# One step of Q computed from one tile on GpSimd, another instruction order, and another order of the first loads

## Chip, cores and metric

The kernel runs on one NeuronCore of a Trainium2 chip. The metric is the device time of one execution in microseconds; lower is better. The engines are TensorE (PE, matrix products, with its weight loads shown as PEld), VectorE (DVE), ScalarE (ACT), GpSimd (POOL) and SyncE (SP, which issues transfers).

## What is computed

An attention over pooled keys, then two MLPs, all in float32. There are 12288 tokens and 128 channels; 768 keys; the MLPs have 2048 hidden units.

```python
kv_pool = kv.reshape(B, H // r, r, W // r, r, C).mean(axis=(2, 4))
k = v = kv_pool.reshape(B, -1, C) @ w_sr          # 768 keys
s = scale * (q @ k.transpose(0, 2, 1))
a = np.exp(s - s.max(-1, keepdims=True)); a /= a.sum(-1, keepdims=True) + 1e-09
x = a @ v
...
r = np.maximum(x @ w1_in, 0.0)                    # first MLP
y = (r * r) @ w1_out
...
h = y @ w2_in; h2 = h * h; h3 = h2 * h            # second MLP
P = a[0] + a[1] * h + a[2] * h2 + a[3] * h3
Q = 1.0 + np.abs(b[0]) * np.abs(h) + np.abs(b[1]) * h2
out = (P / (Q + 1e-06)) @ w2_out
```

## The kernel before

**Tiles.** Channels lie on the 128 partitions and tokens along the row. The tokens are cut into 25 blocks: one of 384, 22 of 512, one of 384 and one of 256. Hidden units are taken 128 at a time (16 rows of hidden units in a block), and the second MLP takes two of them together as a *pair*: 8 pairs in a block, 200 in all, each of 1024 columns in a full block.

**Three-part products.** Where a product needs float32 accuracy, an operand is split into a rounded high part and the low rest (names ending in h or H, and l or L), and three matmuls are added: high by high, high by low, low by high (L805 to L807 for the hidden products of both MLPs, L823 to L825 for some of the output products, L749 to L751 for attention). The other output products are plain float32 (L819), of which the trace has two records for each matmul. L679 are the scores, L720 the transposes of the softmax rows.

**Start.** Sixteen loads bring the keys' samples into one large buffer, `room`; DVE (L482) and POOL (L486) sum 16 samples a key. Small loads bring a and b. DVE decides from them by a flag whether a branch with completed squares (`SQUARES`, `fast=True`) can be taken; it is the one that runs. All engines read the flag and branch. DVE also works out the coefficients (columns of `cf`, 13 small steps), and the weights, which come as float64, are decoded on DVE (L574 to L592).

**Second MLP, a pair.** ACT takes |h| into U (L944) and a square of h into Z (L958). Q, divided by |b1|, goes into K. For the pairs in `qpool` POOL makes it in two steps, `kk` (L947) K = sU + t, and `qp` (L949) K = K · U; for the other pairs ACT squares (L952, `sq2`). ACT then takes ln (L969) and exp (L970) for an approximate 1/Q, and DVE does the cubic (L960), and three steps that refine and multiply (L982, L984, L987). Pairs 0 and 3 are split into mH (ACT or DVE, L997 or L998) and mL (POOL, L1000) for three-part output products.

**First MLP, a row.** Relu on ACT or DVE (L847, L850), the square on ACT or POOL (L853, L856), and for 10 of 16 rows a split, gH on ACT (L865) and gL on POOL (L871). `split` (L782, L779, L785) makes the high and low part of each block's x and y.

**What sets the order.** A planner, `Plan`, is run when the program is built. It has every operation with a priority (16 slots a block, offsets `off` by kind of operation, `lead1` and `leada` for how far the first MLP and attention run ahead), engine alternatives with a penalty in slots (`sq_act`, `sq_pool` and so on), a cost function for each, and the number of buffers and PSUM banks; it plays the work through by these costs and writes the instructions in the order of its starts. Each engine then runs its own instructions in that order.

## Time and profile before

| | |
|---|---|
| median of 3 runs | 1487.1 us (1486.95 to 1488.85) |
| the profiled execution | 1486.91 us, its span 1484.7 us |
| mean granted clock of TensorE | 0.989 |
| instructions in the trace | 18746 |
| TensorE busy | 1439.5 us |
| VectorE, ScalarE, GpSimd busy | 1386.9, 1393.4, 1334.1 us |

The time of an execution is the span of its instructions and about 2 us around it. An engine's busy time is the union of its instructions. A wait counts for the end only where the engine that waits sets the pace at that time; the chain that ended last, which the page follows back from the last instruction, lies on PE for 67% of the span.

### The profile page before, as it was taken

The page shows a single profiled execution, that of the slowest core. Times are in us where ns is not written, and L with a number is a line of the kernel's source. Part 1 is how long each engine was busy: PE and PEld are TensorE (multiplying, and loading weights), DVE is VectorE, ACT ScalarE, POOL GpSimd, SP SyncE. Part 2 cuts the span into 40 slices and gives each one's busy share as a digit, 9 for nine tenths or more (in the row PEclk, how much of TensorE's full clock was granted, in tenths as well). Part 3 has the DMA queues.
Part 4 walks back from the last instruction along what each step waited for, and adds up shares of the span by engine and source line. Part 5 has one row for each costly group of instructions (what it writes and reads, how often), then busy time and mean ns, then how long its engine had stood idle before and what let it go on. Part 6 is the DMA issues. An engine that isn't in the chain of part 4 may idle for free.

```text
span 1484.7 us, 18746 instructions
## 1 busy us (share of the span) xinstructions
PE 1439.5 (97%) x5991; PEld 1053.8 (71%) x5991; DVE 1386.9 (93%) x1857; ACT 1393.4 (94%) x2318; POOL 1334.1 (90%) x1021
## 2 busy tenths in 40 slices
PE   5999999999999999999999999999999999999986
PEld 4887767766767777776777777777777777767764
DVE  7999999999999999999999999999989899989998
ACT  3789989999999999999999999999999999999996
POOL 4789999998999899999998997989999999889984
PEclk8999999999999999999999999999999999999998
DMA  7310000000000000000000000000000000000000
GB/s 283 114 36 8 13 0 15 14 2 8 15 8 15 8 3 13 15 8 8 8 15 8 1 15 15 8 8 15 8 8 8 8 13 1 11 5 3 8 8 12
DMA packets 15549, 28.62 MB, mean 19 GB/s; under 512 B 1745, under 2 KB 6737, under 8 KB 15441
## 3 DMA queue, kind: packets, MB, share of 16 engines
q1 hardware_dynamic: 15440, 27.34, 5.5%
...
## 4 chain that ended last, share of the span: by engine, by line
PE 67%; POOL 13%; ACT 8%; DVE 7%; issue 3%; DMA 1%; SPq 0%; POOLq 0%; ACTq 0%; DVEq 0%
PE psum L819 17%; PE psum L805 9%; PE psum L806 8%; PE psum L807 8%; PE psum L679 4%; PE psum L824 4%; POOL room L949 4%; PE psum L825 4%; PE psum L823 4%; PE psum L720 4%; POOL gL L871 3%; POOL room L947 2%; POOL room L856 2%; PE psum L750 1%; PE psum L749 1%
## 5 line engine op out<-in xcount | busy, mean ns | idle before, releaser
L949 POOL TENSOR_TENSOR room<-room 128x1024 f32<-128x1024 f32 (+2 forms) x150 | 348.3, 2322 | 3.6
L871 POOL TENSOR_TENSOR gL<-room,gH 128x512 fp32r<-128x512 f32 (+2 forms) x250 | 313.0, 1262 | 20.8 <-PE psum L824 15.8
L960 DVE SCALAR_TENSOR_TENSOR room<-room,cf,psum 128x512 f32<-128x512 f32 (+2 forms) x400 | 279.5, 720 | 17.4 <-ACT room L958 15.8
L819 PE MATMUL psum<-room,w1o 128*128 128x512 f32 (+2 forms) x600 | 285.2, 583 | 4.0 <-DVE room L987 4.0
L856 POOL TENSOR_TENSOR room<-room 128x512 f32<-128x512 f32 (+2 forms) x261 | 262.3, 1022 | 12.5 <-ACT room L847 6.6
L982 DVE SCALAR_TENSOR_TENSOR room<-room,v,psum 128x1024 f32<-128x1024 f32 (+2 forms) x200 | 246.1, 1232 | 21.2 <-ACT psum L970 19.4
L958 ACT ACTIVATE room<-psum,cf 128x512 f32<-128x512 f32 (+2 forms) x400 | 262.8, 688 | 0.0
L969 ACT ACTIVATE room<-room,cf 128x1024 f32<-128x1024 f32 (+2 forms) x200 | 226.3, 1132 | 25.4 <-POOL room L949 24.8
L984 DVE SCALAR_TENSOR_TENSOR psum<-room,cf,psum 128x1024 f32<-128x1024 f32 (+2 forms) x200 | 247.5, 1238 | 0.0
L987 DVE SCALAR_TENSOR_TENSOR room<-psum,room 128x1024 f32<-128x1024 f32 (+2 forms) x200 | 235.2, 1177 | 3.1
L944 ACT ACTIVATE room<-psum 128x512 f32<-128x512 f32 (+2 forms) x400 | 223.4, 593 | 12.5 <-PE psum L807 6.5
L947 POOL TENSOR_SCALAR room<-room,cf 128x1024 f32<-128x1024 f32 (+2 forms) x150 | 164.7, 1098 | 48.3 <-ACT room L944 36.0
L970 ACT ACTIVATE psum<-room 128x1024 f32<-128x1024 f32 (+2 forms) x200 | 202.7, 1015 | 0.7 <-DVE room L960 0.3
L805 PE MATMUL psum<-yh,w1h 128*128 128x512 f32 (+2 forms) x400 | 191.2, 478 | 4.8 <-DVE room L987 3.5
L805 PE MATMUL psum<-xh,w0h 128*128 128x512 f32 (+2 forms) x400 | 182.8, 457 | 1.6 <-DVE xh L782 1.2
L819 PEld LDWEIGHTS psum<-room,w1o 128*128 128x128 f32 x600 | 111.1, 192 | 63.1 <-issue 42.9
L806 PE MATMUL psum<-xl,w0h 128*128 128x512 f32 (+2 forms) x400 | 153.4, 383 | 1.5 <-DVE xl L785 1.2
L807 PE MATMUL psum<-yh,w1l 128*128 128x512 f32 (+2 forms) x400 | 154.2, 386 | 0.0
L806 PE MATMUL psum<-yl,w1h 128*128 128x512 f32 (+2 forms) x400 | 153.9, 385 | 0.0
L807 PE MATMUL psum<-xh,w0l 128*128 128x512 f32 (+2 forms) x400 | 153.6, 384 | 0.0
L847 ACT ACTIVATE room<-psum 128x512 f32<-128x512 f32 (+2 forms) x255 | 148.3, 601 | 5.1 <-PE psum L807 3.2
L865 ACT ACTIVATE gH<-room 128x512 fp32r<-128x512 f32 (+2 forms) x250 | 149.8, 632 | 2.9 <-POOL room L856 2.6
...
## 6 DMA issues: line engine op xcount, KB each, us to landing
...
```

Of the source, the lines that this page charges most:

```text
L805: nc.tensor.matmul(out=out, lhsT=w_hi[m][:, sl], rhs=hi, start=True, stop=False)
L806: nc.tensor.matmul(out=out, lhsT=w_hi[m][:, sl], rhs=lo, start=False, stop=False)
L807: nc.tensor.matmul(out=out, lhsT=w_lo[m][:, sl], rhs=hi, start=False, stop=True)
L819: nc.tensor.matmul(out=o, lhsT=w_o[m][:, place[m][fi], :], rhs=rhs(), start=first, stop=last)
L856: nc.gpsimd.tensor_tensor(out=G(), in0=G(), in1=G(), op=ALU.mult)
L871: nc.gpsimd.tensor_tensor(out=mk("gL", gl)[:, :T], in0=G(), in1=f(tiles[gh][:, :T]), op=ALU.subtract)
L949: one("qp", POOL, c_pool, lambda v: nc.gpsimd.tensor_tensor(out=v(ku), in0=v(ku), in1=v(uu), op=ALU.mult), None, [uu], [ku])
L958: one("sP", ACT, ptr(c_actp), lambda v: act(out=v(zz), in_=v(hh), func=AF.Square, bias=co["c"]), "Z", [hh])
L960: one("z3", DVE, ptr(c_dve), lambda v: stt(out=v(zz), in0=v(zz), scalar=co["nd"], in1=v(hh), op0=ALU.subtract, op1=ALU.mult), None, [hh], ...
L982: one("g0", DVE, ptr(c_dve), lambda v: stt(out=v(zz), in0=v(zz), scalar=e0, in1=v(yy), op0=ALU.add, op1=ALU.mult), None, [yy], [zz])
L984: one("tt", DVE, c_dl, lambda v: stt(out=v(yy), in0=v(ku), scalar=dl, in1=v(yy), op0=ALU.add, op1=ALU.mult), None, [ku], [yy])
L987: one("g2", DVE, c_dve, lambda v: stt(out=v(g_), in0=v(yy), scalar=2.0, in1=v(zz), op0=ALU.subtract, op1=ALU.mult, reverse0=True), None, [ ...
```

## The change

It has four parts. First, in the branch that runs, POOL's two steps on Q become K = √QS · U + k1 and K = K · K, a linear step times itself; what is missing from Q is one constant, `da`, which ACT's ln and DVE's refinement add as they added another constant, `dp`, before. ACT's version of Q already had this form, so `da` now serves all pairs, and two coefficients are not needed any more. Second, the last two blocks have a set of pairs of their own that POOL takes (`qtail`): 0, 3, 4, 5, 6, 7, where the other blocks have 0, 1, 3, 4, 5, 7. Third, the planner has a cost of its own for the new step and a floor for three-part products, and nearly all of its numbers (buffers, banks, leads, penalties, offsets) are others. Fourth, ScalarE's queue issues b, a and `wsr`, so that the key loads come first on SyncE's; and the coefficients are worked out after the branch, as an operation of the plan.

```diff
-        qr=1, qh=1, ql=1, e=4, mn=17, sm=21, aT=1, xh=2, xl=1, yh=2, yl=2, aH=3, aL=2, g1=8, U=2, K=3, Z=7, o=1,
-        gH=6, gL=3, mH=1, mL=1,
+        qr=1, qh=1, ql=1, e=5, mn=27, sm=29, aT=1, xh=2, xl=1, yh=2, yl=2, aH=3, aL=2, g1=8, U=2, K=3, Z=7, o=1,
+        gH=5, gL=3, mH=1, mL=1,
...
-        h2=6, yb=5, sc=6, st=6, x=1, h1=5, y1=1, y2=1, dc=1,
+        h2=4, yb=6, sc=6, st=5, x=1, h1=6, y1=1, y2=1, dc=1,
...
-    lead1=17.5,
+    lead1=20.5,
...
     qpool=[0, 1, 3, 4, 5, 7],
-    sq_act=8,
-    sq_pool=0.5,
+    qtail=[0, 3, 4, 5, 6, 7],
+    sq_act=0,
+    sq_pool=8,
...
-        mh2=-266.25, mh1=-79.25, sc=-10.0, tr=0.75, nr=-368.25, g2=7.0, ex=-137.5, kk=-177.25, rl=-4.75,
+        mh2=-164.5, mh1=-75.5, sc=-71.0, tr=1.0, nr=-376.25, g2=37.0, ex=-126.75, kk=-258.0, rl=23.75, tt=120.0,
...
 def c_mm3(n):
-    return 3 * (0.4375 * n + 6)
+    return 3 * max(0.4375 * n + 6, 110)
...
+def c_poolq(n):
+    return 1.96 * n + 10
...
-        rem, spl, spd, qpool = fp in REM, fp in SPL, fp in SPD, fp in QPOOL or not fast
+        rem, spl, spd, qpool = fp in REM, fp in SPL, fp in SPD, not fast or fp in (QPOOL if b < NB - 2 else QTAIL)
...
-            s1, s2 = (QS, co["k2"]) if fast else (co["b"][:, 1:2], co["b"][:, 0:1])
+            s1, s2 = (QS ** 0.5, co["k1"]) if fast else (co["b"][:, 1:2], co["b"][:, 0:1])
             one("kk", POOL, c_pools, lambda v: ts(
                 out=v(ku), in0=v(uu), scalar1=s1, scalar2=s2, op0=ALU.mult, op1=ALU.add), "K", [uu])
-            one("qp", POOL, c_pool, lambda v: nc.gpsimd.tensor_tensor(
-                out=v(ku), in0=v(ku), in1=v(uu), op=ALU.mult), None, [uu], [ku])
+            qf = ku if fast else uu
+            one("qp", POOL, c_poolq if fast else c_pool, lambda v: nc.gpsimd.tensor_tensor(
+                out=v(ku), in0=v(ku), in1=v(qf), op=ALU.mult), None, [uu], [ku])
...
-        dl = (co["dp"] if qpool else co["da"]) if fast else QC
+        dl = co["da"] if fast else QC
...
+            P.op(-9, (DVE, 1500.0, co["make"], 0), new=[("const", "co")])
...
-    nc.sync.dma_start(out=ab[:, 0:4], in_=pa.to_broadcast([128, 4]))
-    nc.sync.dma_start(out=ab[:, 4:6], in_=pb.to_broadcast([128, 2]))
-    nc.sync.dma_start(out=wsr, in_=w_sr)
+    nc.scalar.dma_start(out=ab[:, 4:6], in_=pb.to_broadcast([128, 2]))
+    nc.scalar.dma_start(out=ab[:, 0:4], in_=pa.to_broadcast([128, 4]))
+    nc.scalar.dma_start(out=wsr, in_=w_sr)
...
-    ts(c1(t, 6), c1(t, 5), -1.0, 1.0, MUL, ADD)
+    def squares():
+
+        ts(c1(t, 6), c1(t, 5), -1.0, 1.0, MUL, ADD)
```

What the numbers do is seen in the instructions' order. Line numbers of the new program are 6 or 7 higher at the same code. Three places follow.

VectorE around the branch, before: the last coefficients, the flag's load, the branch, and the first key sums (L482).

```order
L1146 SCALAR_TENSOR_TENSOR cf<-cf,v 128x1
L1117 TENSOR_SCALAR cf<-t 128x1
L1151 SCALAR_TENSOR_TENSOR cf<-cf 128x1
L1117 TENSOR_SCALAR cf<-ab,r 128x1
L1117 TENSOR_SCALAR cf<-cf 128x1
L1138 TENSOR_LOAD flag
L1159 COMPARE_AND_BRANCH
L482 TENSOR_REDUCE room<-room 128x48 x12
L515 SCALAR_TENSOR_TENSOR k_lo<-psum,k_hi 128x384
```

VectorE around the branch, now: the flag, the branch, and then the coefficients; the last four steps of them and then the key sums (L488, twelve again) follow the piece.

```order
L1145 CAST flag<-t 128x1
L1146 TENSOR_LOAD flag
L1171 COMPARE_AND_BRANCH
L1125 TENSOR_SCALAR t<-t 128x1
L1151 SCALAR_TENSOR_TENSOR r<-ab,t 128x1
L1152 SCALAR_TENSOR_TENSOR r<-m,t 128x1
L1153 RECIPROCAL r<-r 128x2
L1125 TENSOR_SCALAR v<-ab,r 128x3
L1125 TENSOR_SCALAR cf<-v 128x1
L1156 SCALAR_TENSOR_TENSOR cf<-cf,v 128x1
L1125 TENSOR_SCALAR t<-m,r 128x1
L1125 TENSOR_SCALAR cf<-t 128x1
```

The coefficients have moved behind the branch and still stand ahead of the first key sum.

TensorE in the 13th block's attention, before: transposes of two groups of keys, hidden products of both MLPs, and then a group's product with V (L749 to L751), which belongs to the group transposed one place earlier than the first row here.

```order
L720 MATMUL psum<-ident,room 128x128 x4
L819 MATMUL psum<-room,w0o 128x512
L720 MATMUL psum<-ident,room 128x128 x4
L805 MATMUL psum<-xh,w0h 128x512
L806 MATMUL psum<-xl,w0h 128x512
L807 MATMUL psum<-xh,w0l 128x512
L805 MATMUL psum<-yh,w1h 128x512
L806 MATMUL psum<-yl,w1h 128x512
L807 MATMUL psum<-yh,w1l 128x512
L749 MATMUL psum<-aH,v_hi 128x512
L750 MATMUL psum<-aL,v_hi 128x512
L751 MATMUL psum<-aH,v_lo 128x512
```

TensorE at the same place now.

```order
L726 MATMUL psum<-ident,room 128x128 x4
L825 MATMUL psum<-room,w0o 128x512
L825 MATMUL psum<-room,w1o 128x512 x2
L811 MATMUL psum<-yh,w1h 128x512
L812 MATMUL psum<-yl,w1h 128x512
L813 MATMUL psum<-yh,w1l 128x512
L811 MATMUL psum<-yh,w1h 128x512
L812 MATMUL psum<-yl,w1h 128x512
L813 MATMUL psum<-yh,w1l 128x512
L755 MATMUL psum<-aH,v_hi 128x512
L756 MATMUL psum<-aL,v_hi 128x512
L757 MATMUL psum<-aH,v_lo 128x512
```

The product with V now follows the transposes of its own group, with nine matmuls between them.

VectorE from the last split of y on (yl of the block with 256 tokens), before.

```order
L785 TENSOR_TENSOR yl<-psum,yh 128x256
L984 SCALAR_TENSOR_TENSOR psum<-room,cf,psum 128x2x384
L960 SCALAR_TENSOR_TENSOR room<-room,cf,psum 128x384 x2
L987 SCALAR_TENSOR_TENSOR room<-psum,room 128x2x384
L982 SCALAR_TENSOR_TENSOR room<-room,v,psum 128x2x384
L984 SCALAR_TENSOR_TENSOR psum<-room,cf,psum 128x2x384
L987 SCALAR_TENSOR_TENSOR room<-psum,room 128x2x384
L982 SCALAR_TENSOR_TENSOR room<-room,v,psum 128x2x384
L960 SCALAR_TENSOR_TENSOR room<-room,cf,psum 128x384 x2
L984 SCALAR_TENSOR_TENSOR psum<-room,cf,psum 128x2x384
L987 SCALAR_TENSOR_TENSOR room<-psum,room 128x2x384
L982 SCALAR_TENSOR_TENSOR room<-room,v,psum 128x2x384
```

VectorE from the same split on, now: L967 is the cubic (L960 before), L989, L991 and L994 the three steps on whole pairs (L982, L984 and L987).

```order
L791 TENSOR_TENSOR yl<-psum,yh 128x256
L991 SCALAR_TENSOR_TENSOR psum<-room,cf,psum 128x2x384
L967 SCALAR_TENSOR_TENSOR room<-room,cf,psum 128x384 x2
L994 SCALAR_TENSOR_TENSOR room<-psum,room 128x2x384
L989 SCALAR_TENSOR_TENSOR room<-room,v,psum 128x2x384
L991 SCALAR_TENSOR_TENSOR psum<-room,cf,psum 128x2x384
L994 SCALAR_TENSOR_TENSOR room<-psum,room 128x2x384
L989 SCALAR_TENSOR_TENSOR room<-room,v,psum 128x2x384
L967 SCALAR_TENSOR_TENSOR room<-room,cf,psum 128x256 x3
L991 SCALAR_TENSOR_TENSOR psum<-room,cf,psum 128x2x384
L989 SCALAR_TENSOR_TENSOR room<-room,v,psum 128x2x256
L967 SCALAR_TENSOR_TENSOR room<-room,cf,psum 128x256
```

Before, 66 steps follow that split, 24 of them on single rows (8 of 384 tokens and 16 of 256); now 50 follow, 18 of them on single rows (2 of 384 and 16 of 256). TensorE has 120 matmuls left behind the last output product of the first MLP before, and 92 now.

## Rows read from the trace of the kernel before

**Rows 1.** The page's first part: busy us, share of the span, instructions.

```profile
PE 1439.5 (97%) x5991; PEld 1053.8 (71%) x5991; DVE 1386.9 (93%) x1857; ACT 1393.4 (94%) x2318; POOL 1334.1 (90%) x1021
```

**Rows 2.** Stretches: length; busy us (instructions) of each engine; granted clock, DMA share, GB/s.

```profile
0.00:60.00 60.00, 40.61 (x212) 36.03 (x213) 51.34 (x127) 30.07 (x65) 33.75 (x42) 0.89 0.64 222
60.00:1400.00 1340.00, 1331.53 (x5488) 967.30 (x5488) 1259.95 (x1626) 1292.53 (x2113) 1242.96 (x925) 1.00 0.03 11
1400.00:1430.00 30.00, 29.19 (x146) 22.26 (x145) 29.09 (x36) 29.35 (x57) 29.46 (x33) 1.00 0.03 9
1430.00:1485.00 55.00, 38.17 (x150) 28.25 (x148) 46.52 (x71) 41.48 (x86) 27.94 (x24) 0.83 0.03 8
```

**Rows 3.** Waits of PE, 60 to 1400 us: total us, times, longest.

```profile
PE psum L824 <- POOL mL L1000: 1.8, 4, 0.8
PE psum L806 <- DVE xl L785: 1.2, 1, 1.2
```

**Rows 4.** Groups by shape, POOL: busy us, mean ns | idle before, its releaser.

```profile
L949 POOL TENSOR_TENSOR room<-room 128x1024 f32<-128x1024 f32 x132 | 318.5, 2413 | 2.7
L871 POOL TENSOR_TENSOR gL<-room,gH 128x512 fp32r<-128x512 f32 x220 | 284.6, 1304 | 18.2 <-PE psum L824 14.5
...
L856 POOL TENSOR_TENSOR room<-room 128x512 f32<-128x512 f32 x232 | 241.5, 1057 | 12.3 <-ACT room L847 6.6 <-DVE room L850 1.9
...
L856 POOL TENSOR_TENSOR room<-room 128x256 f32<-128x256 f32 x14 | 8.6, 637 | 0.2
```

**Rows 5.** Groups by shape, PE and ACT.

```profile
L806 PE MATMUL psum<-xl,w0h 128*128 128x512 f32 x352 | 138.0, 392 | 1.2 <-DVE xl L785 1.2
...
L853 ACT ACTIVATE room<-room 128x512 f32<-128x512 f32 x120 | 74.6, 649 | 1.0 <-DVE room L850 0.8
```

**Rows 6.** Order of time, SP's queue, first 24 us: start, us, instruction.

```profile
0.74 0.39 SPq L1106 DMA_DIRECT2D ab<-in_moe_a_dram  x1
...
2.12 12.30 SPq L1111 DMA_DIRECT2D room<-in_kv_dram  x16
```

**Rows 7.** Order of time, DVE, first 24 us: start, us, instruction [idle before].

```profile
5.25 0.17 DVE L1121 SCALAR_TENSOR_TENSOR m<-ab 128x6 f32<-128x6 f32 x1 [1.67 <-DMA ab<-in_moe_b_dram]
...
6.74 0.15 DVE L1137 CAST flag<-t 128x1 int32<-128x1 f32 x1
...
9.19 0.14 DVE L1117 TENSOR_SCALAR cf<-cf 128x1 f32<-128x1 f32 x1
10.01 5.50 DVE L482 TENSOR_REDUCE room<-room 128x48 f32<-128x384 f32 x8 [0.68 <-issue]
16.05 1.41 DVE L482 TENSOR_REDUCE room<-room 128x48 f32<-128x768 f32 x2 [0.54 <-DMA room<-in_kv_dram]
```

**Rows 8.** The chain that ended last, from 1395 us: start, us, what.

```profile
1400.09 0.23 PE psum L805
...
1418.80 0.86 PE psum L819 x2
...
1476.50 4.69 PE psum L819 x12
```

**Rows 9.** Order of time, DVE, 1430 to 1440 us.

```profile
1433.17 0.42 DVE L785 TENSOR_TENSOR yl<-psum,yh 128x256 fp32r<-128x256 f32 x1
```

**Rows 10.** Groups by shape, DVE, blocks of 384 tokens.

```profile
L960 DVE SCALAR_TENSOR_TENSOR room<-room,cf,psum 128x384 f32<-128x384 f32 x32 | 18.7, 609 | 1.6 <-ACT room L958 1.0 <-PE psum L819 0.5
...
L984 DVE SCALAR_TENSOR_TENSOR psum<-room,cf,psum 128x768 f32<-128x768 f32 x16 | 16.2, 1015 | 0.0
...
L987 DVE SCALAR_TENSOR_TENSOR room<-psum,room 128x768 f32<-128x768 f32 x16 | 15.2, 953 | 0.2
```

**Rows 11.** Waits of all engines, whole span: total us, times, longest.

```profile
ACT room L969 <- POOL room L949: 24.8, 43, 1.7
...
PEld psum L749 <- DVE aL L740: 3.2, 8, 0.7
...
PEld psum L750 <- DVE aL L740: 2.9, 8, 0.9
```

More of the change, by code (lines that the diff above doesn't have):

```diff
@@ L48 @@
     rem=[],
-    md_act=1,
-    md_dve=60,
-    rl_act=8,
+    md_act=60,
+    md_dve=0.5,
+    rl_act=0,
     rl_dve=2,
     qh_act=4,
-    qh_dve=1,
+    qh_dve=0.5,
     spd=[],
@@ L63 @@
     mh_dve=0,
-    ml_pool=0,
+    ml_pool=2,
     ml_dve=60,
     ev_dve=8,
-    hi_dve=0,
+    hi_dve=1,
     rg=1,
@@ L74 @@
     off=dict(
-        mh2=-266.25, mh1=-79.25, sc=-10.0, tr=0.75, nr=-368.25, g2=7.0, ex=-137.5, kk=-177.25, rl=-4.75,
-        tt=85.5, ev=79.75, mo2=10.5, ln=49.75, g0=-38.25, ab=3.5, sq=184.75, y0=14.75, mn=-278.0, qp=100.0,
-        av=-119.5, mo1=4.25, sP=85.5, sq2=132.5, rr=198.5, mh=-16.5, ml=-198.75,
+        mh2=-164.5, mh1=-75.5, sc=-71.0, tr=1.0, nr=-376.25, g2=37.0, ex=-126.75, kk=-258.0, rl=23.75, tt=120.0,
+        ev=33.75, mo2=10.5, ln=114.25, g0=-10.5, ab=-80.5, sq=186.75, y0=-21.5, mn=-380.5, qp=185.5, av=-140.25,
+        mo1=3.0, sP=130.0, sq2=158.5, rr=199.75, mh=-170.25, ml=-210.25,
     ),
@@ L112 @@
     qpool=[],
+    qtail=[],
     sq_act=4,
@@ L441, in program @@
     w_lo = [const.tile([128, DFF], F32R, name=f"w{m}l") for m in range(2)]
-    REM, SPL, SPD, QPOOL = CFG["rem"], CFG["spl"], CFG["spd"], CFG["qpool"]
+    REM, SPL, SPD, QPOOL, QTAIL = CFG["rem"], CFG["spl"], CFG["spd"], CFG["qpool"], CFG["qtail"]
     HS = [[fi for k in ks for fi in (2 * k, 2 * k + 1)] for ks in (CFG["hs"], sorted(REM + SPL + SPD))]
@@ L936, in mlp2 @@
             P.op(p + off("mh2"), (PE, len(es) * c_mm3(T), mh, 0), new=[("h2", hh[e]) for e in es] + ([(n, (n, b, fp)) for n in "UZ"] if 0 in es else []),
-                 rd=[("yh", b), ("yl", b)] + [(w, 1, G * fp + e) for e in es for w in ("wh", "wl")]
+                 rd=["co", ("yh", b), ("yl", b)] + [(w, 1, G * fp + e) for e in es for w in ("wh", "wl")]
                  + ([] if 0 in es else [("U", b, fp)]))
@@ L1138, in attn_moe_moe, with terms @@
     fits = nc.values_load(flag[0:1, 0:1], min_val=0, max_val=1)
-    ts(c1(t, 6), c1(t, 5), -1.0, 1.0, MUL, ADD)
-    V.scalar_tensor_tensor(out=c1(r, 0), in0=c1(ab, 3), scalar=c1(t, 5), in1=c1(t, 6), op0=MUL, op1=ADD)
-    V.scalar_tensor_tensor(out=c1(r, 1), in0=c1(m, 5), scalar=c1(t, 5), in1=c1(t, 6), op0=MUL, op1=ADD)
-    V.reciprocal(out=r, in_=r)
-    ts(v, ab[:, 0:3], c1(r, 0), None, MUL)
-    ts(c1(co_f, 0), c1(v, 2), 0.5, None, MUL)
-    V.scalar_tensor_tensor(out=c1(co_f, 1), in0=c1(co_f, 0), scalar=c1(co_f, 0), in1=c1(v, 1), op0=MUL, op1=SUB)
-    ts(c1(t, 7), c1(m, 4), c1(r, 1), 0.5, MUL, MUL)
-    ts(c1(co_f, 2), c1(t, 7), QS ** 0.5, None, MUL)
-    ts(c1(co_f, 3), c1(t, 7), 2.0 * QS, None, MUL)
-    ts(c1(co_f, 4), c1(r, 1), QC, None, MUL)
-    V.scalar_tensor_tensor(out=c1(co_f, 5), in0=c1(co_f, 2), scalar=c1(co_f, 2), in1=c1(co_f, 4), op0=MUL, op1=SUB)
-    ts(c1(co_f, 5), c1(co_f, 5), -1.0, None, MUL)
-    ts(c1(co_f, 6), c1(ab, 3), c1(r, 1), QS, MUL, MUL)
-    ts(co_g[:, 0:4], ab[:, 0:4], QS, None, MUL)
-    ts(co_g[:, 4:6], m[:, 4:6], QS, None, MUL)
-    V.memset(c1(co_g, 6), QC)
+    def squares():
+        ts(c1(t, 6), c1(t, 5), -1.0, 1.0, MUL, ADD)
+        V.scalar_tensor_tensor(out=c1(r, 0), in0=c1(ab, 3), scalar=c1(t, 5), in1=c1(t, 6), op0=MUL, op1=ADD)
+        V.scalar_tensor_tensor(out=c1(r, 1), in0=c1(m, 5), scalar=c1(t, 5), in1=c1(t, 6), op0=MUL, op1=ADD)
+        V.reciprocal(out=r, in_=r)
+        ts(v, ab[:, 0:3], c1(r, 0), None, MUL)
+        ts(c1(co_f, 0), c1(v, 2), 0.5, None, MUL)
+        V.scalar_tensor_tensor(out=c1(co_f, 1), in0=c1(co_f, 0), scalar=c1(co_f, 0), in1=c1(v, 1), op0=MUL, op1=SUB)
+        ts(c1(t, 7), c1(m, 4), c1(r, 1), 0.5, MUL, MUL)
+        ts(c1(co_f, 2), c1(t, 7), QS ** 0.5, None, MUL)
+        ts(c1(co_f, 4), c1(r, 1), QC, None, MUL)
+        V.scalar_tensor_tensor(out=c1(co_f, 5), in0=c1(co_f, 2), scalar=c1(co_f, 2), in1=c1(co_f, 4), op0=MUL, op1=SUB)
+        ts(c1(co_f, 5), c1(co_f, 5), -1.0, None, MUL)
+        ts(c1(co_f, 6), c1(ab, 3), c1(r, 1), QS, MUL, MUL)
+    def terms():
+        ts(co_g[:, 0:4], ab[:, 0:4], QS, None, MUL)
+        ts(co_g[:, 4:6], m[:, 4:6], QS, None, MUL)
+        V.memset(c1(co_g, 6), QC)
     args = (room, wsr, qT, kvT, w1_in, w1_out, w2_in, w2_out, outT)
@@ L1160, in attn_moe_moe @@
         with ExitStack() as c:
-            co = dict(c=c1(co_f, 0), nd=c1(co_f, 1), e=c1(v, 0), k1=c1(co_f, 2), k2=c1(co_f, 3), dp=c1(co_f, 4),
+            co = dict(make=squares, c=c1(co_f, 0), nd=c1(co_f, 1), e=c1(v, 0), k1=c1(co_f, 2),
                       da=c1(co_f, 5), out=c1(co_f, 6))
@@ L1165, in attn_moe_moe @@
         with ExitStack() as c:
-            co = dict(a=co_g[:, 0:4], e=c1(co_g, 0), b=co_g[:, 4:6], qc=c1(co_g, 6))
+            co = dict(make=terms, a=co_g[:, 0:4], e=c1(co_g, 0), b=co_g[:, 4:6], qc=c1(co_g, 6))
             program(c, tc, TERMS, False, co, *args)
```

## The prediction

> **What bounds the kernel now.** I read the page's busy shares first. TensorE (PE) is busy 97% of the span, ScalarE (ACT) 94, VectorE (DVE) 93, GpSimd (POOL) 90 [rows 1]. Four engines this full leave one question: where is PE not busy? The stretches answer it [rows 2]. PE is idle 60 − 40.6 = 19.4 us in the first 60, 1340 − 1331.5 = 8.5 us in the next 1340, and 0.8 + 16.8 = 17.6 us after 1400. That makes 45.5 of 1484.7 us, 19% of it in the long middle. So there are three regimes. At the start PE waits for keys and decoded weights, with DVE busy 51.3 of 60 us. In the middle PE sets the pace, and DVE, ACT and POOL have 6, 4 and 7% to spare. At the end nothing but the second MLP is left and DVE sets the pace: it is busy 29.1 of 30 and 46.5 of 55 us while PE has 38 of 55.
>
> What PE waits for in the middle is spread thin: the largest releaser, POOL's low part of a gated pair, has 1.8 us in four times, the next, one split of DVE's, 1.2 [rows 3], and ten smaller ones follow. No single one carries the 8.5 us.
>
> The change leaves PE's work alone: the two orders hold the same 5484 matmuls, form by form. So a microsecond saved on POOL or ACT counts only where it ends one of these three idle times. The busy share hides some waits: a record of a 512-column matmul lasts 0.39 us [rows 5], but they start 0.23 apart [rows 8], so a wait under 0.16 us shows as busy. Summing start distances over all matmuls I estimate about 1406 us of own work for PE, and some 20 us lost in the middle instead of 8.5.
>
> **Part 1, Q as a linear step times itself.** POOL's second step on Q reads one tile twice instead of two tiles; the first step keeps its form. No row has it at 1024 columns. From above: the squares of the first MLP, also a tile times itself, take 1057 ns at 512 columns and 637 at 256 [rows 4], and twice 1057 is 2.11 us. From below: 1057 + 512 × (1057 − 637)/256 = 1.90 us. The old step takes 2.41 [rows 4]. That two different sources are dearer is seen at 512 columns as well, 1304 against 1057. I take 2.0, between the two, as both come from the same kind of step. Saving 0.41 × 132 = 54 us, and about 6 more on the 18 smaller ones by the same scaling: 60 us of POOL (bounds 45 to 74). The Trainium skill speaks against this part (GPSIMD Engine Reference, Elementwise — side-by-side cycle accounting): a two-input step runs at about 2.6 cycles per element because both operands share one read port, which would hold for a tile times itself too, and the saving would be nought. The trace differs, 1057 against 1304 at the same 512 columns; By the rule POOL would stand at 1359 us instead of about 1300 after part 2, and the time where rival 3 has it.
>
> **Part 2, the searched order.** Counted in the two orders: 26 squares of the first MLP move from ACT (22 at 649 ns [rows 5]) to POOL (22 at 1057); eleven more splits of yh and xh go to DVE from ACT; four conversions of q and four of mH go from DVE to ACT. Worked through with the mean of each form: ACT −17 us, POOL +25 for the squares, DVE +2. With part 1, POOL goes 1334 − 60 + 25 = 1299 (bounds 1285 to 1314; 1359 without the saving), ACT 1393 to 1376, DVE 1387 to 1389. All of it lies beside PE's work in the middle, at cost nought as long as PE has its operands; if a queue slips, the price is PE's wait.
>
> Does the new order give PE more cover? I walked along PE's order and added 0.23 us for each matmul of a three-part product and 0.86 for a whole plain one of 512 columns [rows 8]. From a pair's hidden product to its output product PE has a median of 27.8 us of own work before and 35.7 after; from the first MLP's last output to the second's first hidden product 8.1 and 10.8; from scores to transposes 9.3 and 12.4. From a transposed group to its product with V it is the other way, 4.3 before and 3.5 after: the order shows the product right behind its own group now. So the long chain over ACT, POOL and DVE gets a quarter more cover and a short chain over ACT and DVE gets less. I take −3 us, a good third of the idle time seen, with bounds −8.5 (all of it) and +6 (rival 2 in part).
>
> **Part 3, the end.** After the last split of y (yl of the 256-token block, now at 1433.2 [rows 9]) the old order has 120 matmuls and 66 DVE steps left, the new one 92 and 50. The DVE steps that moved ahead are, at 384 tokens, six of 609 ns and nine on whole pairs of 953 to 1015 [rows 10] and one conversion of some 0.5 us, together 13 us. The PE work that moved ahead is 24 parts of three-part products at 0.17 (0.23 × 384/512) and 4 plain ones at 0.65 (0.86 × 384/512 [rows 8]), 6.7 us. If PE sets the pace up to that split, the split comes 6.7 us later and the rest is 13 us shorter: −6.5. If DVE sets it already, DVE's work is only placed differently and the term is nought; DVE at 29.1 of 30 us from 1400 on [rows 2] says that this is nearer. The smaller Q steps shorten POOL's links of the end chain, about 0.3 us each. I take −1.5, between −6.5 and +3 (the end chain's last 4.7 us, twelve records of plain products [rows 8] in a stretch with a mean granted clock of 0.83 [rows 2], can fall at either of the two clock levels).
>
> **Part 4, the start.** The key loads' first issue moves from 2.12 to 0.74 us [rows 6], the place of the first load now. DVE waits for the landings of keys: its pause of 0.54 before the reductions at 16.05 ends with a landing [rows 7], and one of 0.55 follows. The coefficients move behind the branch, but still stand ahead of the first reduction, so DVE does them there: 6.8 to 9.33 (the last begins at 9.19) in the old trace, then 0.68 us to the first reduction at 10.01 [rows 7]. In the new one the flag (6.74 [rows 7]) is followed by that 0.7 and then the 2.4 us of coefficients: 10.0 again, if a and b land as before. They now queue on ScalarE behind no key load, but run beside them; b, issued just ahead of the keys, was waited for until 5.25 [rows 7]. So DVE starts the keys at the same time and loses 1.1 us of waiting: −1.0 us, bounds −2 (the weight loads behind them also come 1.4 earlier) and +2 (a and b land late among the keys, and DVE starts late). All engines stand at the branch until the flag is there, so that price would be whole.
>
> Edits with one answer: the planner's floor of 110 ns changes no cost (a 256-column product is already 118), the pool depths cost nothing by themselves, the dropped coefficients save two steps of 0.15 us.
>
> **Sum.** −1.0 − 3 − 1.5 = −5.5 us. The profiled execution took 1486.9 us (span 1484.7 and 2.2 around it), within 0.2 of the median of the runs, 1487.1; so I forecast 1486.9 − 5.5 = 1481.4, say **1481.5 us**. By the ends of the terms: 1486.9 − 17 = 1470 and 1486.9 + 11 = 1498, neither of which needs all terms at one end to be likely.
>
> **Rivals.**
> 1. *No change.* The waits move and PE's middle loses as much as now; DVE, with 2 us more work, sets the end as before. For it: PE's work is the same to the matmul, the idle time in the middle is 0.6%, and the end is DVE's. Against: more cover for the long chain. Only the start counts, part of it lost: 1486.
> 2. *Slower: products with V right behind their transposes.* In between lie ACT's or DVE's copy out of PSUM and DVE's subtraction. The trace has PE's loads waiting for that subtraction 16 times, 6.1 us in all [rows 11], 0.4 us each. Distances under 3.5 us number 42 of 150 before and 69 after. If the 27 new ones wait 0.4 us each, that is 11 us on PE's path, which nothing takes back in the middle: 1486.9 − 1 + 11 = 1497 with no other gain, 1492 with the gains above. It decides from 0.2 us each, where it eats the 5.5. Against it: PE itself, as opposed to its weight loads, hardly shows this wait.
> 3. *The saving on POOL isn't there.* Then POOL is at 1359 us, 92%, and ACT's waits for its Q (24.8 us in 43 times [rows 11]) grow; PE still has cover in the middle: 1486 to 1489, no change by measure. Chance 0.05, kept within rival 1. The page of the Trainium skill named in part 1 would have it so.
>
> **How the numbers follow.** What a measurement of this kernel can tell from no change is about 0.2%, 3 us: faster is under 1484.1, slower above 1490.1. The forecast (gains in the middle and at the start outlast the short distances) gets 0.55, rival 1 with rival 3 gets 0.26, rival 2 gets 0.19. Range for 8 in 10: 1473, the forecast with half of the middle's remainder and the end's −6.5, up to 1491, where rival 2 at 0.4 us a time with the gains just lies outside. Faster 0.55, same 0.26, slower 0.19.
>
> **What would show it.** Part 1: the new Q step at 1.9 to 2.1 us for 1024 columns and POOL near 1300 us. Part 2: PE's idle time from 60 to 1400 near 5 us, fewer waits of ACT for POOL's Q; rival 2 by more waits of PE's loads for DVE's subtraction. Part 3: the last yl nearer to the end, about 40 us ahead of it instead of 51, and DVE still over 90% busy after 1400. Part 4: first key issue at 0.7 us, first reduction at 10.0, the k product about 1 us earlier. I am wrong if the order costs PE more in the middle than it loses now, if the end grows, or if a and b land so late that the branch does.

## The result and the profile after

The kernel after took 1473.8 us (median of 4 runs, 1471.8 to 1474.5) against 1487.2 (1486.95 to 1488.85): a ratio of 0.9905, 95% interval 0.9892 to 0.9917, 13.4 us less. The forecast was 1481.5, so 8 us of the gain had not been foreseen. The span went from 1484.7 to 1471.6 us. The page of after, its busy shares and the first line on the chain that ended last:

```profile
PE 1430.0 (97%) x5991; PEld 1052.8 (72%) x5991; DVE 1385.5 (94%) x1859; ACT 1385.6 (94%) x2289; POOL 1278.0 (87%) x1044
...
PE 89%; DVE 6%; ACT 2%; issue 1%; DMA 1%; POOL 1%; ACTq 0%; SPq 0%; DVEq 0%; POOLq 0%
```

TensorE's share of the chain rose from 67 to 89%, and GpSimd's fell from 13 to 1%. GpSimd did 56 us less work [rows 1]. The stretches of after, with the columns of [rows 2]:

```profile
0.00:60.00 60.00, 37.73 (x200) 32.62 (x201) 49.22 (x116) 27.82 (x59) 30.00 (x37) 0.91 0.60 210
60.00:1400.00 1340.00, 1338.87 (x5550) 980.56 (x5550) 1272.46 (x1653) 1296.88 (x2107) 1205.35 (x964) 1.00 0.04 11
1400.00:1430.00 30.00, 26.11 (x122) 18.49 (x120) 29.52 (x39) 29.56 (x59) 23.35 (x27) 1.00 0.03 9
1430.00:1472.00 42.00, 27.33 (x122) 21.13 (x122) 34.27 (x55) 31.35 (x67) 19.35 (x19) 0.89 0.03 11
```

From 60 to 1400 us PE is idle 1340 − 1338.9 = 1.1 us; it was 8.5 [rows 2]. As the prediction says, busy hides small waits, so I use its other measure throughout: the start distances of all matmuls add up to 1406.0 us of own work, the same in every kernel here, and how late PE is against this sum can be read at any point. *Start* is its lateness at 100 us of own work, *middle* what comes on from there to 1340, *end* the rest.

| kernel | start | middle | end | sum |
|---|---|---|---|---|
| before | 28.9 | 20.6 | 29.2 | 78.7 |
| after | 31.5 | 7.0 | 27.1 | 65.6 |
| difference | +2.6 | −13.6 | −2.1 | −13.1 |
| forecast | −1.0 | −3 | −1.5 | −5.5 |

Each row stands for one profiled execution, and executions of one kernel lie 1 to 4 us apart, so one or two microseconds in a column say little. The end came near its forecast, the start went the other way, and the middle gave more than four times its term. The experiments ask why for these two. Medians of the kernel before lay between 1487.2 and 1487.8 us in all of them.

### The profile page after: what moved, and what is told of

Same layout as the page of the kernel before. It is cut to its first block, busy times and chain, and to the rows that moved or that the text cites. A ratio compares the mean times of both kernels' runs of the same rounds, so it can differ in the third digit from the quotient of the medians.

```text
span 1471.6 us, 18713 instructions
## 1 busy us (share of the span) xinstructions
PE 1430.0 (97%) x5991; PEld 1052.8 (72%) x5991; DVE 1385.5 (94%) x1859; ACT 1385.6 (94%) x2289; POOL 1278.0 (87%) x1044
## 4 chain that ended last, share of the span: by engine, by line
PE 89%; DVE 6%; ACT 2%; issue 1%; DMA 1%; POOL 1%; ACTq 0%; SPq 0%; DVEq 0%; POOLq 0%
PE psum L825 23%; PE psum L811 11%; PE psum L813 11%; PE psum L812 11%; PE psum L685 6%; PE psum L830 5%; PE psum L831 5%; PE psum L829 5%; PE psum L726 4%; PE psum L755 2%; PE psum L756 2%; PE psum L757 2%; PE psum L759 1%; DVE room L967 1%; DVE psum L991 1%
## 5 line engine op out<-in xcount | busy, mean ns | idle before, releaser
L877 POOL TENSOR_TENSOR gL<-room,gH 128x512 fp32r<-128x512 f32 (+2 forms) x250 | 312.0, 1258 | 37.3 <-PE psum L830 29.1
L862 POOL TENSOR_TENSOR room<-room 128x512 f32<-128x512 f32 (+2 forms) x287 | 288.1, 1020 | 36.0 <-ACT room L853 20.5
L967 DVE SCALAR_TENSOR_TENSOR room<-room,cf,psum 128x512 f32<-128x512 f32 (+2 forms) x400 | 279.1, 719 | 8.6 <-ACT room L965 7.7
L825 PE MATMUL psum<-room,w1o 128*128 128x512 f32 (+2 forms) x600 | 281.6, 578 | 5.7 <-DVE room L994 5.7
L956 POOL TENSOR_TENSOR room<-room 128x1024 f32<-128x1024 f32 (+2 forms) x150 | 274.8, 1833 | 2.6
L989 DVE SCALAR_TENSOR_TENSOR room<-room,v,psum 128x1024 f32<-128x1024 f32 (+2 forms) x200 | 246.1, 1232 | 16.5 <-ACT psum L977 15.7
L991 DVE SCALAR_TENSOR_TENSOR psum<-room,cf,psum 128x1024 f32<-128x1024 f32 (+2 forms) x200 | 247.4, 1237 | 0.0
L950 ACT ACTIVATE room<-psum 128x512 f32<-128x512 f32 (+2 forms) x400 | 223.2, 586 | 18.1 <-PE psum L813 13.5
L994 DVE SCALAR_TENSOR_TENSOR room<-psum,room 128x1024 f32<-128x1024 f32 (+2 forms) x200 | 235.1, 1175 | 2.6
L811 PE MATMUL psum<-xh,w0h 128*128 128x512 f32 (+2 forms) x400 | 179.1, 448 | 0.2 <-DVE room L994 0.2
```

The lines of the kernel that those rows point to most:

```text
L811: nc.tensor.matmul(out=out, lhsT=w_hi[m][:, sl], rhs=hi, start=True, stop=False)
L825: nc.tensor.matmul(out=o, lhsT=w_o[m][:, place[m][fi], :], rhs=rhs(), start=first, stop=last)
L862: nc.gpsimd.tensor_tensor(out=G(), in0=G(), in1=G(), op=ALU.mult)
L877: nc.gpsimd.tensor_tensor(out=mk("gL", gl)[:, :T], in0=G(), in1=f(tiles[gh][:, :T]), op=ALU.subtract)
L956: one("qp", POOL, c_poolq if fast else c_pool, lambda v: nc.gpsimd.tensor_tensor(out=v(ku), in0=v(ku), in1=v(qf), op=ALU.mult), None, [uu] ...
L967: one("z3", DVE, ptr(c_dve), lambda v: stt(out=v(zz), in0=v(zz), scalar=co["nd"], in1=v(hh), op0=ALU.subtract, op1=ALU.mult), None, [hh], ...
```

## Which part made the middle: the step or the order?

My theory was the prediction's: the new order gives the long chain more cover, and the cheaper Q step lies beside PE's work at no gain. The rival: the step alone is the gain. Two kernels take one part each.

**The step alone.** The order of all engines is that of before.

```diff
-            s1, s2 = (QS, co["k2"]) if fast else (co["b"][:, 1:2], co["b"][:, 0:1])
+            s1, s2 = (QS ** 0.5, co["k1"]) if fast else (co["b"][:, 1:2], co["b"][:, 0:1])
...
+            qf = ku if fast else uu
...
-                out=v(ku), in0=v(ku), in1=v(uu), op=ALU.mult), None, [uu], [ku])
+                out=v(ku), in0=v(ku), in1=v(qf), op=ALU.mult), None, [uu], [ku])
...
-        dl = (co["dp"] if qpool else co["da"]) if fast else QC
+        dl = co["da"] if fast else QC
```

> The old kernel with POOL's second step on Q as K times K (and the constant da for all pairs), in the old instruction order, row for row on every engine. Of the 13.1 us by which the span fell, the middle (from 100 to 1340 us of TensorE's own work) gave 13.6. Theory A, the order: the new order's longer cover ended TensorE's waits, and the quicker step alone ends only those on POOL, 2.4 for the low parts and 1.4 for the normalised rows: 1484 us (1482 to 1486). Rival B, the step: 66 us less on POOL shorten the chain to 1/Q for every pair whatever the order: 1477 us or less, with TensorE idle under 3 us from 60 to 1400.

Measured: 1474.7 us, ratio 0.9915 (0.9898 to 0.9931); start 29.2, middle 9.4, end 28.2. My theory fell: this one step in the old order takes 11.2 of the middle's 13.6 us. ScalarE's ln, which waited 24.8 us for Q before [rows 11], hardly waits now (total us, times, longest):

```profile
ACT room L970 <- POOL room L950: 3.1, 6, 1.0
```

**The order alone**: the program of after with K · U, `k2` and `dp` as before.

```diff
-            s1, s2 = (QS ** 0.5, co["k1"]) if fast else (co["b"][:, 1:2], co["b"][:, 0:1])
+            s1, s2 = (QS, co["k2"]) if fast else (co["b"][:, 1:2], co["b"][:, 0:1])
...
-            qf = ku if fast else uu
+            qf = uu
...
-        dl = co["da"] if fast else QC
+        dl = (co["dp"] if qpool else co["da"]) if fast else QC
...
```

> The new kernel, its order unchanged on PE, ACT and POOL (two more coefficient steps on DVE ahead of the keys), with the old second step K times U at 2.41 us. Theory A, the order: 1475 to 1478 us, since the cover of 36 us from hidden to output product takes the half microsecond more of each Q; POOL at 1344 us is busy 91%. Rival B, the step: the waits come back, 1484 us or more.

Measured: 1517.2 us, ratio 1.0201 (1.0184 to 1.0218); start 31.9, middle 48.0, end 29.9. With the old step the new order is 43 us slower than after, and 30 slower than before. Its waits over the whole span (total us, times, longest):

```profile
ACT room L976 <- POOL room L956: 60.8, 85, 2.0
...
PE psum L811 <- ACT room L853: 4.6, 7, 1.4
```

ScalarE's ln stands 60.8 us for Q, and behind it in ScalarE's queue stand the relus of the first MLP, for which PE then waits. After has only 2.8 us of the first (its row is shown below). So more cover by count, 35.7 against 27.8 us, was no cover at all where Q came late.

## What does the step save: GpSimd's time, or ScalarE's wait for Q?

Half a microsecond less in each of 132 steps does two things: every later step of GpSimd's queue comes earlier, and Q itself is ready earlier. Small squares on a tile of their own, `pad`, which nobody reads, put GpSimd's time back without touching Q.

**Old order, refilled in one step** of 180 columns (100 in the smaller blocks) behind the second step on Q:

```diff
+            pad = co["pad"][:, :180 if T == 512 else 100] if fast else None
...
+                nc.gpsimd.tensor_tensor(out=v(ku), in0=v(ku), in1=v(qf), op=ALU.mult)
+                if fast:
+                    nc.gpsimd.tensor_tensor(out=pad, in0=pad, in1=pad, op=ALU.mult)
```

> The kernel before with the quick second step on Q in its old order (measured 1474.7 us), and directly behind that step in GpSimd's queue a step of about 0.5 us on a small tile of its own that nobody reads. So GpSimd is as full as with the old step, but Q is ready 0.5 us earlier. Theory 'queue' (what counted was GpSimd's time: every later step in its queue came 0.5 us later): the gain is gone, 1484 to 1488. Theory 'chain' (what counted was the time from |h| to ln): 1474 to 1477. In between, both.

Measured: 1488.2 us, ratio 1.0008 (0.9998 to 1.0017), middle 20.1. That looked like the queue, but VectorE was busy 1404.2 us, 19 more than with the step alone. Two of its forms, the conversions whose input and output lie both in SBUF (groups by shape: busy us, mean ns):

```profile
L1004 DVE CAST mH<-room 128x1024 fp32r<-128x1024 f32 x22 | 36.6, 1664 | 0.9 <-PE psum L825 0.4
...
L652 DVE CAST qh<-room 128x512 fp32r<-128x512 f32 x10 | 19.1, 1909 | 1.2 <-PE psum L679 1.1
```

In the kernel before they took 980 and 1059 ns, with the step alone 1099 and 1108; here some wait through a whole row of GpSimd's steps. One of them, in order of time, first GpSimd, then VectorE:

```profile
308.31 1.32 POOL L871 TENSOR_TENSOR gL<-room,gH 128x512 fp32r<-128x512 f32 x1
309.56 1.92 POOL L953 TENSOR_TENSOR room<-room 128x1024 f32<-128x1024 f32 x1
311.42 0.51 POOL L955 TENSOR_TENSOR pad<-pad 128x180 f32<-128x180 f32 x1
312.56 2.39 POOL L1006 TENSOR_TENSOR mL<-room,mH 128x1024 fp32r<-128x1024 f32 x1 [0.63 <-DVE mH L1004]
```

```profile
309.05 3.42 DVE L1004 CAST mH<-room 128x1024 fp32r<-128x1024 f32 x1
312.40 1.27 DVE L988 SCALAR_TENSOR_TENSOR room<-room,v,psum 128x1024 f32<-128x1024 f32 x1
```

The conversion begins at 309.05 and ends at 312.47, 0.54 us behind the end of the last of three GpSimd steps that follow each other without a gap, and GpSimd then waits 0.63 us for its result. So this run may have a second cause, and the next one takes it away.

**Old order, refilled in two steps** of 30 columns each (`for _ in range(2)` in full blocks, one step in the smaller ones, on a `pad` of 30 columns).

> As the old order refilled (1488.2 us), but GpSimd's extra half microsecond is two steps of 0.24 us on 30 columns instead of one of 0.50 on 180. In that run VectorE's conversions into mH, whose input and output lie in SBUF, had grown from 1.10 to 1.66 us, which gives a second cause beside the queue. Theory 'queue' (GpSimd's later steps came later): again 1484 to 1488, with the conversions at 1.0 to 1.2 us. Theory 'conversions' (VectorE was held up by GpSimd's unbroken run of steps): 1475 to 1479.

Measured: 1474.5 us, ratio 0.9911 (0.9895 to 0.9928); start 29.1, middle 9.4. GpSimd, groups by shape, and VectorE's conversions:

```profile
L953 POOL TENSOR_TENSOR room<-room 128x1024 f32<-128x1024 f32 x132 | 252.3, 1912 | 2.5
...
L955 POOL TENSOR_TENSOR pad<-pad 128x30 f32<-128x30 f32 x282 | 69.2, 245 | 10.3
```

```profile
L1004 DVE CAST mH<-room 128x1024 fp32r<-128x1024 f32 x22 | 22.6, 1027 | 0.9 <-PE psum L825 0.4
...
L652 DVE CAST qh<-room 128x512 fp32r<-128x512 f32 x10 | 11.7, 1173 | 1.3 <-PE psum L679 1.1
```

GpSimd is busy 1316.6 us, 62 more than with the step alone, and nothing is lost. So in the old order GpSimd's share of the time wasn't what the step saved, and the 13.5 us of the one-step refill go with VectorE's conversions: 22 of them 0.64 us longer and ten 0.74 longer make 21 us of VectorE's time. Why one filler shuts them out and two shorter ones don't is open.

**Half of it**, one step of 30 columns:

> The old order with the quick second step (1474.7 us, GpSimd 1255 us) and one step of 0.24 us behind it, so GpSimd at about 1291 us, near the middle between that and before (1334, 1487.3). If time grows with GpSimd's work: 1474.7 + 12.6 x 36/79 = 1480.4, 1479 to 1482. If there is a margin and then a fall: under 1477.

Measured: 1475.1 us, ratio 0.9912 (0.9895 to 0.9928), GpSimd 1283.8 us. No proportion to GpSimd's time, as the run above would have it.

**New order, refilled behind the step** and, in the second kernel, **between the linear step and the product**, where Q is late too; again two steps in full blocks and one in the smaller ones. The first kernel, and then the second:

```diff
+            def qstep(v):
+                nc.gpsimd.tensor_tensor(out=v(ku), in0=v(ku), in1=v(qf), op=ALU.mult)
+                for _ in range((2 if T == 512 else 1) if fast else 0):
+                    nc.gpsimd.tensor_tensor(out=pad, in0=pad, in1=pad, op=ALU.mult)
...
+            def qstep(v):
+                for _ in range((2 if T == 512 else 1) if fast else 0):
+                    nc.gpsimd.tensor_tensor(out=pad, in0=pad, in1=pad, op=ALU.mult)
+                nc.gpsimd.tensor_tensor(out=v(ku), in0=v(ku), in1=v(qf), op=ALU.mult)
```

> The kernel after (1473.8 us) with two small steps of together about 0.5 us on a tile of their own directly behind the second step on Q in GpSimd's queue. With the old, dearer second step this order took 1517. Theory 'queue': 1508 to 1520, as with the old step. Theory 'chain': 1474 to 1480, and ScalarE's ln waits for GpSimd as little as after (2.8 us).

> The kernel after with the two small steps (0.48 us together) ahead of the second step on Q instead of behind it (1485.8 us). GpSimd's queue is as full, but Q is ready 0.5 us later. If only the queue counts: 1484 to 1488, and the 1517 us with the old step come from its further 17 us of GpSimd's work. If the chain from |h| to ln counts in this order: 1500 to 1515, and ScalarE's ln waits for GpSimd 45 us or more instead of 17.8.

Measured: 1485.8 us, ratio 0.9986 (0.9976 to 0.9996), behind the step; 1492.2, ratio 1.0032 (1.0019 to 1.0045), in front of it. Both theories had a share: the fill alone costs 12.0 us in this order, which has less room, and Q's lateness by its place another 6.4. Neither reached the 1500 and more that it had named. The waits of ln for Q, first kernel and second:

```profile
ACT room L981 <- POOL room L959: 17.8, 31, 1.3
```

```profile
ACT room L981 <- POOL room L961: 32.3, 59, 1.5
```

**Half of the second step left out**: in full blocks it squares only the first 512 of 1024 columns, so half of Q stays linear.

```diff
-                out=v(ku), in0=v(ku), in1=v(qf), op=ALU.mult), None, [uu], [ku])
+                out=v(ku)[:, 0:1] if T == 512 else v(ku), in0=v(ku)[:, 0:1] if T == 512 else v(ku),
+                in1=v(qf)[:, 0:1] if T == 512 else v(qf), op=ALU.mult), None, [uu], [ku])
```

> The kernel after with the second step on Q done for the first 512 of 1024 columns only, so half of Q stays linear: about 0.85 us less on each of 132 steps, some 112 us of GpSimd's time. If GpSimd still holds the pace after the change, another 5 us or more go: 1469 or less, and TensorE's lateness in the middle (7 us) falls. If the quick step already ended its part, 1472 to 1474: the saving has had its whole effect.

Measured: 1472.2 us (1471.8 to 1472.6), ratio 0.9897 (0.988 to 0.9913), GpSimd 1166.2 us. Another 112 us off GpSimd bring 1.6 us, which the runs' spread nearly covers. The quick step had had its whole effect.

One column goes with the time through all of these, with one exception:

| kernel | GpSimd busy | ln waits for Q | time |
|---|---|---|---|
| step alone, old order | 1255.0 | 3.1 in 6 | 1474.7 |
| half refill, old order | 1283.8 | 3.1 in 6 | 1475.1 |
| two-step refill, old order | 1316.6 | 4.1 in 6 | 1474.5 |
| one-step refill, old order (conversions) | 1321.5 | 4.1 in 7 | 1488.2 |
| before | 1334.1 | 24.8 in 43 | 1487.3 |
| half second step, new order | 1166.2 | 1.4 in 3 | 1472.2 |
| after | 1278.0 | 2.8 in 5 | 1473.8 |
| refill behind, new order | 1338.6 | 17.8 in 31 | 1485.8 |
| refill in front, new order | 1334.7 | 32.3 in 59 | 1492.2 |
| old step, new order | 1355.7 | 60.8 in 85 | 1517.2 |

Against the quick step in the same order each us of this wait goes with 0.6 to 0.8 us of time: (1487.3 − 1474.7)/(24.8 − 3.1) = 0.58, and 0.80, 0.62 and 0.75 for the last three rows. ScalarE, 94% busy, works in order, so most of what it loses there is lost. In the last three kernels of the table VectorE was busy 1386.8 to 1390.4 us, against 1385.5 after, so longer conversions are not the cause there.

**What stays open.** That Q's lateness costs time is shown in the new order by the two places of one fill. In the old order the two-step refill and the kernel before make such a pair. By busy time the refill fell 17 us short of the kernel before, but busy time leaves out the gap between the two small steps. From the start of the second step to the start of the next step on other data, where that follows without a wait, GpSimd's queue is held 2.36 us before, 1.85 with the step alone and 2.37 with the two-step refill (medians of full blocks). So in full blocks the queue is as full as before, but Q is ready 0.57 us earlier (3.87 against 4.44 us from the start of the linear step to the end of the product, mean of 150), and the 13 us are saved. The same small steps in front of the product were not tried there. Nor do the runs say why the old step costs 25 us more than the fill in front of the new one: Q is only some 0.1 us later (4.72 against 4.59 us) and the queue is held as long (2.36 against 2.37).

## The start

**All small loads first on SyncE again**, with the coefficients behind the branch, and in a second kernel ahead of it, as before. The first two lines and the last two are in the second kernel alone:

```diff
-            P.op(-9, (DVE, 1500.0, co["make"], 0), new=[("const", "co")])
+            P.op(-9, (DVE, 1500.0, lambda: None, 0), new=[("const", "co")])
...
-    nc.scalar.dma_start(out=ab[:, 4:6], in_=pb.to_broadcast([128, 2]))
-    nc.scalar.dma_start(out=ab[:, 0:4], in_=pa.to_broadcast([128, 4]))
-    nc.scalar.dma_start(out=wsr, in_=w_sr)
+    nc.sync.dma_start(out=ab[:, 0:4], in_=pa.to_broadcast([128, 4]))
+    nc.sync.dma_start(out=ab[:, 4:6], in_=pb.to_broadcast([128, 2]))
+    nc.sync.dma_start(out=wsr, in_=w_sr)
...
+    squares()
+    terms()
```

> The new kernel with a, b and the sampling weights first on SyncE's queue again; the coefficients stay behind the branch. Theory C: b and a landed 3.4 us late among the keys (DVE waited until 8.60, before until 5.25) and that held all engines at the branch: flag at 6.7 us again, first key sum near 12, 1471 us (2 to 3 us less than the new kernel). Rival D: the coefficients behind the branch made the start late, not the landing: 1473 to 1474, no gain.

> The new kernel with the whole old start: a, b, weights first on SyncE, coefficients ahead of the branch; order otherwise unchanged. TensorE stood 2.6 us later at 100 us of its own work in the new kernel than in the old; with the old start it stands as early as in the old: 1470 to 1471 us by theory C and by rival D alike; over 1472.5 would mean that the start is made up for later and costs the end nothing.

Measured: 1469.7 us (1468.2 to 1472.4), ratio 0.9883 (0.9866 to 0.9899), and 1470.2 (1469.6 to 1471.3), ratio 0.9887 (0.9871 to 0.9904). Both beat before and after; the place of the coefficients makes no difference that can be told, the place of the loads some 4 us. The start of after, in order of time:

```profile
0.73 0.41 ACTq L1114 DMA_DIRECT2D ab<-in_moe_b_dram  x1
0.74 14.18 SPq L1119 DMA_DIRECT2D room<-in_kv_dram  x16
1.17 0.46 ACTq L1115 DMA_DIRECT2D ab<-in_moe_a_dram  x1
...
8.60 0.17 DVE L1129 SCALAR_TENSOR_TENSOR m<-ab 128x6 f32<-128x6 f32 x1 [8.60 <-DMA ab<-in_moe_a_dram]
...
10.08 0.15 DVE L1145 CAST flag<-t 128x1 int32<-128x1 f32 x1
...
11.45 1.04 DVE L1152 SCALAR_TENSOR_TENSOR r<-m,t 128x1 f32<-128x1 f32 x1
11.48 3.82 POOL L492 TENSOR_TENSOR room<-room 128x384 f32<-128x384 f32 x4
...
14.78 0.54 DVE L1160 SCALAR_TENSOR_TENSOR cf<-cf 128x1 f32<-128x1 f32 x1
...
15.54 8.00 DVE L488 TENSOR_REDUCE room<-room 128x48 f32<-128x384 f32 x12
...
20.96 0.91 PE L513 MATMUL psum<-room,wsr 128*128 128x384 f32 x2 [2.08 <-DVE room L488]
```

b and a are issued by 1.6 us, but a, among the key loads, is waited for until 8.60; the flag, the branch and all engines wait for it. Then the coefficients run while GpSimd sums keys, and single steps on one column take 0.5 to 1.04 us instead of about 0.2. The same in the kernel with the old start:

```profile
0.74 0.39 SPq L1114 DMA_DIRECT2D ab<-in_moe_a_dram  x1
...
5.17 0.17 DVE L1129 SCALAR_TENSOR_TENSOR m<-ab 128x6 f32<-128x6 f32 x1 [1.61 <-DMA ab<-in_moe_b_dram]
...
6.66 0.15 DVE L1145 CAST flag<-t 128x1 int32<-128x1 f32 x1
...
9.94 5.58 DVE L488 TENSOR_REDUCE room<-room 128x48 f32<-128x384 f32 x8 [0.69 <-DVE cf L1125]
...
15.57 0.91 PE L513 MATMUL psum<-room,wsr 128*128 128x384 f32 x2
```

There the key sums begin at 9.94 and the k product at 15.57. Against this after is 5.6 us later at the sums and 5.4 at the product; 3.6 us of it are left in the time (1473.8 − 1470.2). At the end of the last key sum it is 3.9 us (27.04 against 23.10), since with the old start later sums wait for landings of keys, 0.53 and 0.55 us, and in after the first twelve run without a wait.

The Trainium skill (DMA: Bandwidth & Descriptors, Issuing engines are not separate DMA queues) says that transfers of several issuing engines run on the same 16 DMA engines and interleave. The trace agrees: on a queue of their own these loads landed 3.4 us later than ahead of the keys on the same queue.

**The loads moved in the kernel before**, nothing else:

> The kernel before with b, a and the sampling weights on ScalarE's queue, nothing else. In the kernel after this move cost 4 us (1473.8 against 1469.7). If the cost is the start's own, all engines standing at the branch: 1490 to 1492 here, the flag near 10 us (6.74 before). If the new program only dislikes it: 1486 to 1488.

Measured: 1489.8 us, ratio 1.0010 (1.0000 to 1.0019), against 1487.8; start 31.3 instead of 28.9. VectorE:

```profile
8.88 0.17 DVE L1121 SCALAR_TENSOR_TENSOR m<-ab 128x6 f32<-128x6 f32 x1 [8.01 <-DMA ab<-in_moe_a_dram]
...
10.36 0.15 DVE L1137 CAST flag<-t 128x1 int32<-128x1 f32 x1
...
13.63 8.01 DVE L482 TENSOR_REDUCE room<-room 128x48 f32<-128x384 f32 x12 [0.67 <-DMA room<-in_kv_dram]
```

The flag is 3.6 us later (6.74 before [rows 7]) and so are the sums; 2 us of that remain, just under the range expected and at the edge of the runs' noise. So the branch's lateness costs something in the old program too, less than the 4 us in the new one.

**a and b first on SyncE, `wsr` on ScalarE, coefficients behind the keys**:

```diff
-        def vlo(part=part, j0=j0, js=js):
+        def vlo(part=part, j0=j0, js=js, h=h):
+            if h == 1:
+                co["make"]()
...
-            P.op(-9, (DVE, 1500.0, co["make"], 0), new=[("const", "co")])
+            P.op(-9, (DVE, 1500.0, lambda: None, 0), new=[("const", "co")])
...
-    nc.scalar.dma_start(out=ab[:, 4:6], in_=pb.to_broadcast([128, 2]))
-    nc.scalar.dma_start(out=ab[:, 0:4], in_=pa.to_broadcast([128, 4]))
+    nc.sync.dma_start(out=ab[:, 4:6], in_=pb.to_broadcast([128, 2]))
+    nc.sync.dma_start(out=ab[:, 0:4], in_=pa.to_broadcast([128, 4]))
```

> The kernel after with b and a first on SyncE's queue again, ahead of the keys, the sampling weights left on ScalarE's, and the coefficients made behind the last low part of the keys instead of right behind the branch. With all three small loads first on SyncE the time was 1469.7, with the coefficients ahead of the branch 1470.2. If VectorE's start of the key sums sets the start: sums begin about 8 us (10.0 before) and the time is 1467 to 1469. If the landings of the keys set it: 1469.5 to 1471, no change. If wsr lands late among the keys: later than 1471.

Measured: 1472.9 us, ratio 0.9903 (0.9886 to 0.9919), 3 us worse than with all small loads first on SyncE, wherever the coefficients stood. VectorE:

```profile
6.05 0.17 DVE L1131 SCALAR_TENSOR_TENSOR m<-ab 128x6 f32<-128x6 f32 x1 [6.05 <-DMA ab<-in_moe_a_dram]
...
7.53 0.15 DVE L1147 CAST flag<-t 128x1 int32<-128x1 f32 x1
10.01 5.37 DVE L488 TENSOR_REDUCE room<-room 128x48 f32<-128x384 f32 x8 [2.33 <-POOL room L492]
...
26.61 0.15 DVE L1127 TENSOR_SCALAR t<-t 128x1 f32<-128x1 f32 x1
...
28.46 0.88 DVE L1162 SCALAR_TENSOR_TENSOR cf<-cf 128x1 f32<-128x1 f32 x1
```

b and a land at 6.05, 0.85 us later than with `wsr` behind them in one queue (5.20). The sums don't begin before 10.01, as the first of them waits for GpSimd's first sum, and 3 us of coefficients now stand among VectorE's decoding of weights. The first product with `wsr` waits for nothing, so its load is not what is late. It seems that the cheap place for the coefficients is where VectorE would wait anyway; the two moves were not made one by one. I know no better start than the old one.

## Why the prediction was right and wrong

The kernel is faster, as forecast, but 1473.8 us lies at the very edge of the range of 1473 to 1491, and it is there by luck. The range's lower end was made of more cover from the order and 6.5 us at the end; what carried the time there is GpSimd's quicker step, which the prediction had at nought. In one sum: the step alone took 12.6 us (1487.3 to 1474.7), the rest of the change with the old start 4.5 more (to 1470.2), and the new start gave 3.6 back.

- **What bounds the kernel**: right. PE sets the pace from 60 us on; its idle time there was what could be won.
- **Part 1, the step's length**: 1.90 us, the lower bound; I took 2.0.

```profile
L956 POOL TENSOR_TENSOR room<-room 128x1024 f32<-128x1024 f32 x132 | 250.6, 1900 | 1.7
...
L956 POOL TENSOR_TENSOR room<-room 128x768 f32<-128x768 f32 x12 | 18.0, 1499 | 0.4
```

It saves 132 × 0.513 = 68 us and about 6 on the smaller ones, 74 and not 60; GpSimd stands at 1278 us, where I had 1299 with bounds 1285 to 1314. The page of the Trainium skill cited in part 1 (GPSIMD Engine Reference, Elementwise — side-by-side cycle accounting), as part 1 reads it, would have a tile times itself cost as much as two tiles; the trace says 1900 against 2413 ns, so rival 3 fell.
- **Part 2, "beside PE's work, at cost nought"**: this is the step that failed. GpSimd's saving was 11.2 of the middle's 13.6 us. The middle's −13.6 lies beyond even my bound of −8.5: I had taken the idle time by busy records for all that could be won, though I had put the loss at some 20 us myself. The row that told it stood among those I read: ScalarE's ln waiting 24.8 us for Q [rows 11]. I used it for a rival only, since no wait of PE named GpSimd's Q [rows 3]. What the runs show in its place: time goes with ln's wait for Q at 0.6 to 0.8 us for each us. That the loss reaches PE through ScalarE's queue is seen with the old step in the new order, where PE waits for the relus; in the kernel before it is argued, as PE's own list has no such wait of size. The order's share came out near my number, −2.4 where I had −3: from the step alone to after with the old start the middle goes from 9.4 to 7.0. But with the old step the same order made the middle 48.0, so cover was not the reason that I took it for. ScalarE came to 1385.6 us, where I had 1376.
- **Rival 2**: not seen. Waits of after, whole span, with the one of ln between:

```profile
PEld psum L756 <- DVE aL L746: 3.3, 9, 1.1
...
ACT room L976 <- POOL room L956: 2.8, 5, 0.9
...
PEld psum L755 <- DVE aL L746: 1.3, 4, 0.5
```

The product's weight loads wait 3.3 + 1.3 us for VectorE's subtraction, 3.2 + 2.9 before [rows 11].
- **Part 3, the end**: right in size, −2.1 us for −1.5, and −1.0 of it comes with the step alone. No run parts the other pairs of the last blocks from the order. The last split of y:

```profile
1433.30 0.42 DVE L791 TENSOR_TENSOR yl<-psum,yh 128x256 fp32r<-128x256 f32 x1
```

It stands 38.3 us ahead of the end, forecast 40, before 51.5 [rows 9]. VectorE is busy 89% of the time after 1400, as before; I had said over 90.
- **Part 4, the start**: wrong in sign, +2.6 for −1.0, a little over the bound of +2. The mechanism of that bound, a and b late among the keys, is what happened; I gave it too little, held its price to be whole where 3.6 of 5.6 us stayed, and did not see that the coefficients would then run beside GpSimd's sums, 4.6 us (10.99 to 15.6) instead of 2.5.
